# Raw q and k in long runs, and a token order that follows: a clustered attention and mixture-of-experts kernel

## The chip, the cores and the metric

The kernel runs on one core of a Trainium2 chip (trn2). The metric is the time of one execution in microseconds of the device, median of the runs; the kernel before takes 701.96 us (three runs, 701.67 to 702.21). TensorE does the matrix products and the 128x128 transposes, VectorE (DVE) and ScalarE (ACT) work on elements, GpSimd (POOL) helps them, and SyncE (SP) issues nearly all DMAs, in one queue. Sixteen DMA engines move the bytes.

## What is computed

Attention in clusters, then a dense layer, then a mixture of experts. The part that the change touches is the attention: 2 batches of 8 heads, 768 tokens, 64 dimensions.

```python
q_assign = argmax(einsum('bhsd,hcd->bhsc', q_n, c_n))      # 16 centroids per head
k_assign = argmax(einsum('bhsd,hcd->bhsc', k_n, c_n))
mask = q_assign[:, :, :, None] == k_assign[:, :, None, :]
scores = where(mask, 0.125 * q @ k.T, -1e9)
attn = softmax(scores)
out = attn @ v
x = out.transpose(0, 2, 1, 3).reshape(B * S, H * D)
h = x @ w_in;  x = (h * sigmoid(h)) @ w_out
out[n] = gate[n] * (relu(x[n] @ w1[e]) @ w2[e])            # e: the expert of token n
```

Nothing in the attention depends on the order of the tokens, as long as q, k, v, the masks and the place of the output use the same one.

## The kernel before

The heads are worked on in eight pairs, two heads at a time; here they are called pair 1 to pair 8 (p = 0 to 7 in the code). Pair 1 is treated apart, to start early: `head` loads its q and k with tokens on the partitions, and TensorE transposes them. For pairs 2 to 8 `quarter` loads q and k so that VectorE can transpose them: q of a pair is four DMAs, one for each head and half of the 64 dimensions, and each goes to 32 partitions of the tile `rawq`. Partition j of the 32 gets, for each of 24 blocks g of 32 tokens, 32 elements of token 32g + j: 768 pieces of 128 bytes for one DMA. The same holds for k (`rawk`). GpSimd scales q by 0.125 in place (`fq`), and `fdt` transposes half of the tokens in 32x32 blocks into `full`, with dimensions on the partitions and tokens along them.

From `full` comes all that the scores need (`prep`, `tr`): a rounded high part and a low part of q and k (QQ, K1, lq, KX), and the cluster of each token, found by products with the centroids and a short chain on VectorE that ends in `clu_0oq`. Parts of these tiles have to lie on other partitions too, so SP copies them from SBUF to SBUF: seven copies a pair (six for pair 1), each of 64 partitions by 768 elements, from line 489, and for pairs 2 to 8 four copies of masks, each to 32 partitions, from line 555. The first scores of a pair need three of the seven copies: QX, QQ and K1 of its first head. In pair 1 SP issues these as first, second and fourth.

The scores of a pair are worked on in twelve chunks of 128 query tokens (`chunk_ops`): products on TensorE (lines 596 and 599), a row maximum on VectorE (618), the exponential on ScalarE (624), a transpose on TensorE (635), copies to SBUF, and then the products with v (701), six chunks of v tokens. The sums of the exponentials are turned over by a round trip through DRAM (`rsc`, then `rb`, lines 688 and 693), and line 706 (`fN`) multiplies by their inverses and writes the result, tokens along the free axis, into `xT`, from which the dense layer reads.

The order of all this is set at build time by a planner (`Sched`): each operation has an engine, a cost and a priority, and each engine gets its instructions in the order that the plan gives. What is planned is not what the chip does: the instructions wait for each other by semaphores. A DMA of SP also waits until the one eight places before it is done, since it takes over that one's semaphore. During the wait for pair 1's first scores TensorE does dummy products (line 304), a fixed number of them, ahead of the first scores in its order:

```python
warm(opts.get("warm2", 20), 1, 217, [scores], 50)
```

`whole` loads v of a pair in pieces of 256 bytes (a token of one head), 128 tokens at a time.

Of the kernel before, what the change touches and what calls it, by code (L numbers as in the profile page):

```python
# [187 lines left out]
P = 128  # L188
B, H, S, D = 2, 8, 768, 64
NPAIR = B * H // 2  # L190
NC6 = S // P
HALF = S // 2
# [28 lines left out]
def alt(engines, fn, n, psum=False, two=False):  # L221

    return [(e, cost(e, n, psum, two), (lambda e=e: fn(e)), e == "Pool" or e == "DVE" and not psum) for e in engines]
# [5 lines left out]
def attention(tc, sc, pools, q, k, v, centroids, ident, xT, opts):  # L229
    nc = tc.nc  # L230
    if True:
# [5 lines left out]
        def sbt(buf, shape, dt=F32, part=""):  # L237
            return pools["a_early" if buf.tag in EARLY else "a_sb"].tile(shape, dt, tag=buf.key + part, name=buf.key + part)

        def pst(buf, shape=(P, 512)):  # L240
            return pools["a_ps"].tile(list(shape), F32, tag=buf.key, name=buf.key)
# [95 lines left out]
        def load(p):  # L337
            b, hp = divmod(p, H // 2)
            r = raws[p] = {}
            base = 12.0 * (p - 1) - 12  # L340
            for n, (nm, src) in enumerate((("q", q), ("k", k), ("v", v))):
                buf = Buf("raw" + nm)

                def whole(src=src, buf=buf):
                    buf.tile = sbt(buf, [P, 2, NC6, D])
                    nc.sync.dma_start(buf.tile, src[b, 2 * hp:2 * hp + 2].rearrange("h (c p) d -> p h c d", c=NC6))

                def head(h, src=src, buf=buf):
                    if h == 0:
                        buf.tile = sbt(buf, [P, NC6, 2 * D])  # L350
                    nc.sync.dma_start(buf.tile[:, :, h * D:(h + 1) * D], src[b, 2 * hp + h].rearrange("(c p) d -> p c d", c=NC6))

                def quarter(a, src=src, buf=buf):
                    if a == 0:
                        buf.tile = sbt(buf, [P, S // 32, 32])
                    half = slice(32 * (a % 2), 32 * (a % 2) + 32)
                    nc.sync.dma_start(buf.tile[32 * a:32 * a + 32], src[b, 2 * hp + a // 2].rearrange("(g j) d -> j g d", j=32)[:, :, half])
                fs = [whole] if nm == "v" else [lambda h=h, f=head: f(h) for h in range(2)] if p == 0 else [lambda a=a, f=quarter: f(a) for a in range(4)]
                pr = base + 0.1 * n + (opts.get("rawp", 5.0) if p > 1 else 0)
                if p == 0 and nm == "v":  # L360
                    pr += opts.get("v0", 11.5)
                elif p == 1 and nm != "v":
                    pr = -23.0 + 0.1 * n
                deps = [raws[p - 1][nm][1]] if p > 1 or p and nm == "v" else []
                o = None
                for k_, f in enumerate(fs):
                    o = op("SP", 475 if p == 0 else 620, f, deps=[o] if k_ else deps, uses=[buf], alloc=[] if k_ else [buf], prio=pr, soft=k_ > 0,
                           xfer=1800 if nm == "v" else 900 if p == 0 else 640)
                    if k_ == 0:
                        start = o  # L370
                r[nm] = (buf, o)
                if p == 0 and nm == "v" or p == 2:
                    wait.append(start)

        def prep(p):

            base = 12.0 * (p - 1)
            hp = p % (H // 2)
# [6 lines left out]
            buf, lq = Buf("opn"), Buf("lq")  # L385
# [13 lines left out]
            if p:  # L399
                rq = raws[p]["q"]  # L400

                def fq():
                    t = rq[0].tile.rearrange("p a i -> p (a i)")
                    nc.gpsimd.tensor_scalar(t, t, 0.125, 1.0, ALU.mult, ALU.mult)
                scaled.append(op("Pool", 882, fq, deps=[rq[1]], uses=[rq[0]], prio=base, gated=True))

            def tr(nm, x, pr):

                rb, ro = raws[p][nm]
                mb, fb = Buf("t"), Buf("full")  # L410
                xs = slice(x * HALF, (x + 1) * HALF)
                HI = "QQ" if nm == "q" else "K1"
                new = [] if his else [buf, lq]

                def ft():
                    mb.tile = pst(mb)
                    for i in range(3):
                        nc.tensor.transpose(mb.tile[:, i * P:(i + 1) * P], rb.tile[:, 3 * x + i], ident)

                def fdt():  # L420
                    fb.tile = sbt(fb, [P, HALF])
                    nc.vector.transpose(fb.tile, rb.tile[:, 12 * x:12 * x + 12].rearrange("p a i -> p (a i)"))

                def fe(e):
                    fb.tile = sbt(fb, [P, HALF])
                    elems(nc, e, fb.tile, mb.tile[:, :HALF], scale=0.125 if nm == "q" else None)

                def fh(e):
                    mk()
                    elems(nc, e, tl[HI][:, :, xs], fb.tile.unsqueeze(1).to_broadcast([P, 2, HALF]))  # L430

                def fl(e):
                    elems(nc, e, tl["lq"][:, xs] if nm == "q" else tl["KX"][:, 0, xs], fb.tile, tl[HI].bitcast(F32)[:, 1, xs], ALU.subtract)

                def flk(h):
                    rs = slice(64 * h, 64 * h + 64)
                    return lambda e: elems(nc, e, tl["KX"][:64, h, xs], fb.tile[rs], tl[HI].bitcast(F32)[rs, 1, xs], ALU.subtract)
                o = ro
                if p == 0:
                    o = op("PE", 327, ft, deps=[o, o_id], uses=[mb, rb], alloc=[mb], prio=pr, gated=True)  # L440
                    o = op(alt(["Act", "DVE"], fe, HALF, psum=True), 0, None, deps=[o], uses=[mb, fb], alloc=[fb], prio=pr)
                else:
                    if nm == "q":
                        o = scaled[0]
                    o = op("DVE", 469, fdt, deps=[o] + (held["masks"] if p == 1 and his else []), uses=[rb, fb], alloc=[fb], prio=pr, gated=True)
                evs.append((fb, o))
                lead = p == 1 and not his
                his[nm, x] = o = op(alt(["DVE", "Act", "Pool"] if p == 0 else ["Act"] if lead else SPLIT_HI, fh, S), 0, None, deps=[o] + list(his.values())[:1] + (held["masks"] if lead else []),
                                    uses=[fb, buf, lq], alloc=new, prio=pr + (2 + 0.1 * (nm == "q") if p == 0 else 0))
                if p == 0 and nm == "k":  # L450
                    los[nm, x] = op(alt(["DVE", "Pool"], flk(0), HALF, two=True), 0, None, deps=[o], uses=[fb] + bufs[nm], prio=pr + 2.2)
                    lo1.append(op(alt(["Pool"], flk(1), HALF, two=True), 0, None, deps=[o], uses=[fb] + bufs[nm], prio=pr + 4.2))
                else:
                    los[nm, x] = op(alt(["DVE", "Pool"] if p == 0 else ["Pool"] if p == 1 and nm == "q" else SPLIT_LO, fl, HALF, two=True), 0, None, deps=[o], uses=[fb] + bufs[nm], prio=pr + (2.2 if p == 0 else 0))
# [126 lines left out]
        def chunk_ops(p, h, c, i, grp, both):  # L581
            o = ops[p]
            t = o["t"]
# [6 lines left out]
            g = i // 3  # L590
# [56 lines left out]
            if i < 2:  # L647

                a = op("PE", 355, fSa, deps=o["first"], uses=[sb, o["buf"]], alloc=[sb], prio=pf("S"), name=f"S{i}")
                a = Sops[i] = op("PE", 355, fSb, deps=[a] + o["ready"][h] + o["mq"][:1], uses=[sb, o["buf"]], prio=pf("S"), name=f"S{i}")  # L650
            else:
                a = Sops[i] = op("PE", 711, fS, deps=o["ready"][h] + o["mq"][:(1 + c // 3) if h == 0 else 4], uses=[sb, o["buf"]], alloc=[sb], prio=pf("S"), name=f"S{i}")
            a = op("DVE", 865, fM, deps=[a], uses=[sb, nb], alloc=[nb], prio=pf("M"), name=f"M{i}")
# [12 lines left out]
            if i % 3 == 2:  # L666
                b, hp = divmod(p, H // 2)
                x = c // 3
                col = x * HALF
                rows = (slice(0, 64), slice(64, 128))  # L670
                if x not in both:
                    both[x] = dict(r=Buf("rr"), grp={}, ops=[])
# [12 lines left out]
                rb, yb, scr = Buf("rb"), Buf("t"), rsc[2 * p + x]  # L685
# [17 lines left out]
                    return f  # L703

                def fN():
                    nc.vector.tensor_tensor(xT[b][hp][:, col:col + HALF].rearrange("m (j p) -> m j p", j=3),  # L706
                                            yb.tile[:, :HALF].rearrange("m (j p) -> m j p", j=3),
                                            rb.tile.rearrange("m p j -> m j p"), ALU.mult)
                r = op("SP", 1100, fW, deps=w["ops"], uses=[w["r"]], prio=pf("W"), xfer=opts["XW"], late=opts["WL"] * (p == 0), name=f"W{i}")
# [9 lines left out]
        i = 0  # L719
# [979 lines left out]
```

## Time and profile before

| | us |
|---|---|
| median of three runs | 701.96 |
| lowest and highest | 701.67, 702.21 |
| the profiled execution | 701.06 |
| its span (first to last instruction) | 699.2 |
| TensorE busy | 684.9 (98%) |
| VectorE busy | 506.8 (72%) |
| ScalarE busy | 416.8 (60%) |
| GpSimd busy | 126.5 (18%) |

The attention takes about the first 230 us; the dense layer and the experts follow. The page of the profile gives busy times by engine. The table of waits says how long an engine stood still for what; the timeline lists the instructions of an engine in order, a number of equal ones in one row, with the idle time before them in brackets; the windows give the busy time of each engine in a stretch, the clock granted to TensorE as a share of full speed, the share of time in which the 16 DMA engines were busy (packets that overlap count twice, so it can exceed 1) and what they moved.

### The profile page before, as it was taken

To read this page: it belongs to the slowest core of one execution; us is meant where nothing else is said; L and a number is where in the kernel's file an instruction comes from. 1 tells how busy PE (TensorE), PEld (TensorE's weight loads), DVE (VectorE), ACT (ScalarE), POOL (GpSimd) and SP (SyncE) were. 2 spreads that over 40 slices of the span, in tenths; PEclk is the share of its full clock that TensorE was granted. 3 is DMA by queue.
4 is the path that set the end of the run, shared out by engine and by line. 5 is a ranking of instruction groups with operands and counts; after the bars stand their busy time and mean duration, and the time that the engine had idled before them with its cause. 6 is when DMAs were issued, how large, how long until landed. Compare 5 with 4: busy or idle time off the path is not lost. (4 is left out here: it accounts for less than half of the span.)

```text
span 699.2 us, 11768 instructions
## 1 busy us (share of the span) xinstructions
PE 684.9 (98%) x4106; PEld 555.6 (79%) x4106; DVE 506.8 (72%) x977; ACT 416.8 (60%) x753; POOL 126.5 (18%) x158
## 2 busy tenths in 40 slices
PE   8999999999999999999999999999999999999995
PEld 7857777677676789999988999999878878787763
DVE  6878898887986789998469353332599888897730
ACT  5956777677777355555343243332555988896740
POOL 5421332232300000000003100000043315221011
PEclk9999999999999999999999999999999999999998
DMA  9964876752620677674204932000022688847740
GB/s 191 182 138 93 177 178 127 156 125 58 151 69 13 184 251 269 191 260 174 98 1 152 358 125 60 31 1 1 0 93 82 198 317 309 318 167 223 279 177 20
DMA packets 104338, 104.82 MB, mean 150 GB/s; under 512 B 70668, under 2 KB 75024, under 8 KB 104272
## 3 DMA queue, kind: packets, MB, share of 16 engines
q1 hardware_dynamic: 101728, 96.56, 48.0%
q0 software_dynamic: 2400, 7.41, 3.1%
q8 instruction: 34, 0.56, 0.4%
q14 instruction: 32, 0.26, 0.1%
q10 hardware_dynamic: 144, 0.03, 0.0%
HBM read 104.99 MB, written 15.17 MB: 172 GB/s over the span
## 5 line engine op out<-in xcount | busy, mean ns | idle before, releaser
L1304 PE MATMUL bank<-whl,whl 128*128 128x384 f32 x768 | 145.7, 338 | 0.6 <-DVE whl L200 0.6
L1304 PEld LDWEIGHTS bank<-whl,whl 128*128 128x128 f32 x768 | 135.5, 188 | 6.4 <-DVE whl L200 1.0
L200 DVE TENSOR_TENSOR whl<-w,whl 128x1024 fp32r<-128x1024 f32 (+2 forms) x100 | 112.6, 1165 | 7.1 <-ACT whl L202 6.4
L624 ACT ACTIVATE p<-big,nm 128x768 f32<-128x768 f32 x96 | 86.8, 905 | 35.2 <-DVE nm L618 33.4
L618 DVE TENSOR_REDUCE nm<-big 128x1 f32<-128x768 f32 x96 | 90.0, 951 | 15.8 <-PE big L599 14.7
L202 ACT ACTIVATE whl<-w 128x1024 fp32r<-128x1024 f32 (+2 forms) x96 | 94.6, 1027 | 8.9 <-DMA w<-in_moe_w_dram 3.1
L635 PE MATMUL t<-ident,p 128*128 128x128 f32 x576 | 75.9, 273 | 1.4 <-DVE w L706 1.4
L635 PEld LDWEIGHTS t<-ident,p 128*128 128x128 f32 x576 | 66.7, 141 | 10.1 <-issue 5.0
L1431 PE MATMUL bank<-whl,xb 128*128 128x512 f32 x288 | 73.2, 400 | 0.0
L1473 PE MATMUL bank<-whl,w 128*128 128x512 f32 x288 | 72.4, 398 | 0.0
L202 ACT ACTIVATE pt<-t 128x384 f32<-128x384 f32 x129 | 58.2, 493 | 20.1 <-PE t L635 20.0
L701 PE MATMUL t<-pt,rawv 128*64 128x384 f32 x384 | 68.3, 494 | 0.0
L1431 PEld LDWEIGHTS bank<-whl,xb 128*128 128x128 f32 x288 | 52.3, 188 | 13.1 <-issue 1.2
L1473 PEld LDWEIGHTS bank<-whl,w 128*128 128x128 f32 x288 | 52.6, 188 | 11.5 <-issue 0.8
L1081 POOL TENSOR_SCALAR row<-L,mx 128x8 f32<-128x8 f32 x12 | 4.6, 383 | 268.5 <-PE bank L1048 143.0
L701 PEld LDWEIGHTS t<-pt,rawv 128*64 128x64 f32 x384 | 25.0, 136 | 31.4 <-issue 31.2
L200 DVE TENSOR_TENSOR whl<-wraw,whl 128x1024 fp32r<-128x1024 f32 x31 | 38.0, 1225 | 15.0 <-ACT whl L202 15.0
L202 ACT ACTIVATE whl<-wraw 128x1024 fp32r<-128x1024 f32 x31 | 32.7, 1057 | 25.7 <-DVE wraw L942 21.9
L1345 PE MATMUL bank<-whl,g_0w 128*128 128x512 f32 x144 | 38.2, 392 | 0.0
L1345 PE MATMUL bank<-whl,g_2w 128*128 128x512 f32 x144 | 37.8, 394 | 0.0
L596 PE MATMUL big<-opn_0K,opn_0QQ 128*128 128x384 f32 x96 | 36.1, 380 | 1.4 <-ACT p L624 0.9
L1345 PE MATMUL bank<-whl,g_1w 128*128 128x512 f32 x144 | 37.2, 392 | 0.0
(301 smaller groups left out, 1095.0 us busy)
## 6 DMA issues: line engine op xcount, KB each, us to landing
w<-in_moe_w_dram SPq DMA_DIRECT2D x88, 512.0 KB
w<-in_moe_w_out_dram SPq DMA_DIRECT2D x8, 1024.0 KB
wraw<-wsc SPq DMA_DIRECT2D x16, 512.0 KB
wsc<-wraw SPq DMA_DIRECT2D x15, 512.0 KB
w<-in_moe_w_in_dram SPq DMA_DIRECT2D x7, 1024.0 KB
wraw<-in_moe_w_dram SPq DMA_DIRECT2D x8, 512.0 KB
x2d<-row SPq DMA_DIRECT2D x12, 260.0 KB
rawv<-in_v_dram SPq DMA_DIRECT2D x8, 384.0 KB
```

The source lines that it names most:

```text
L200: (nc.vector if e == "DVE" else nc.gpsimd).tensor_tensor(dst, a, b, op)
L202: nc.scalar.activation(dst, a, AF.Copy, scale=1.0 if scale is None else scale)
L596: nc.tensor.matmul(sb.tile[:, x, :HALF], t["QQ"][:, h, cs], t["K1"][:, h, sl(x)], start=True, stop=False)
L618: nc.vector.tensor_reduce(nb.tile, sb.tile[:, :, :HALF], AX.XY, ALU.max, negate=True)
L624: nc.scalar.activation(pb.tile.rearrange("p (a b) -> p a b", a=2), sb.tile[:, :, :HALF], AF.Exp, bias=nb.tile[:, 0:1], scale=1.0, accum_ou ...
L635: nc.tensor.transpose(tbs[x].tile[:, j * P:(j + 1) * P], pb.tile[:, kc * P:(kc + 1) * P], ident)
L701: nc.tensor.matmul(yb.tile[rows[z], :HALF], raws[p]["v"][0].tile[:, z, kc], w["grp"][z]["tile"][:, kc], start=(kc == 0), stop=(kc == NC6 - 1))
L1081: nc.gpsimd.tensor_scalar(xb.tile[:, DM:], L[:, j], mx[:, j:j + 1], 1.0, ALU.subtract, ALU.mult)
L1304: nc.tensor.matmul(hb.tile[:, :HALF], w[:, ws, dc, fs], xx[:, s, cs], start=(dc == 0 and n == 0), stop=(dc == 3 and n == 2))
L1345: nc.tensor.matmul(ab.tile, gb.tile[gs][:, js], w[:, ws, fc % 2], start=(fc == 0 and n == 0), stop=(fc == 15 and n == 2))
L1431: nc.tensor.matmul(hbs[x].tile, xs_[:, s, dc], w.tile[:, ws, x * 512:(x + 1) * 512], start=(dc == 0 and n == 0), stop=(dc == 3 and n == 2))
L1473: nc.tensor.matmul(ob.tile, hT.tile[:, s, fc * P:(fc + 1) * P], w.tile[:, ws, i * 512:(i + 1) * 512], start=(fc == 0 and n == 0), stop=(fc ...
```

## The change

Three things change together.

The quarters of q and k are loaded as runs: partition j of the 32 takes tokens 24j to 24j + 23 in one run of 24 x 64 elements less 32, that is 1,504 elements or 6,016 bytes. The run begins at the first or the second half of the dimensions, so of every 64 elements the first 32 are wanted and the other 32 are loaded too and not used. The tiles `rawq` and `rawk` become twice as large; a DMA has 32 runs.

Tokens get another order: place 128c + p along the free axis holds token 6p + c. `fdt` makes this order: it reads blocks at a stride and writes its elements four apart. Pair 1's q and k and all of v are loaded in that order too, so that a partition's six tokens lie next to each other in DRAM; v then has runs of 1,536 bytes. Pair 1's q and k still go to two interleaved places in their tile, in pieces of 256 bytes.

`fN` undoes the order: it writes every sixth element of `xT`, which so keeps the tokens in their own order.

```diff
@@ -343,18 +343,19 @@
 
                 def whole(src=src, buf=buf):
                     buf.tile = sbt(buf, [P, 2, NC6, D])
-                    nc.sync.dma_start(buf.tile, src[b, 2 * hp:2 * hp + 2].rearrange("h (c p) d -> p h c d", c=NC6))
+                    nc.sync.dma_start(buf.tile, src[b, 2 * hp:2 * hp + 2].rearrange("h (p c) d -> p h c d", c=NC6))
 
                 def head(h, src=src, buf=buf):
                     if h == 0:
-                        buf.tile = sbt(buf, [P, NC6, 2 * D])
-                    nc.sync.dma_start(buf.tile[:, :, h * D:(h + 1) * D], src[b, 2 * hp + h].rearrange("(c p) d -> p c d", c=NC6))
+                        buf.tile = sbt(buf, [P, 4 * NC6, D])[:, :2 * NC6].rearrange("p (c h) d -> p c (h d)", h=2)
+                    nc.sync.dma_start(buf.tile[:, :, h * D:(h + 1) * D], src[b, 2 * hp + h].rearrange("(p c) d -> p c d", c=NC6))
 
                 def quarter(a, src=src, buf=buf):
                     if a == 0:
-                        buf.tile = sbt(buf, [P, S // 32, 32])
-                    half = slice(32 * (a % 2), 32 * (a % 2) + 32)
-                    nc.sync.dma_start(buf.tile[32 * a:32 * a + 32], src[b, 2 * hp + a // 2].rearrange("(g j) d -> j g d", j=32)[:, :, half])
+                        buf.tile = sbt(buf, [P, 4 * NC6, D])
+                    at, n = 32 * (a % 2), S * D // 32 - 32
+                    nc.sync.dma_start(buf.tile.rearrange("p a d -> p (a d)")[32 * a:32 * a + 32, :n],
+                                      src[b, 2 * hp + a // 2].rearrange("(j n) d -> j (n d)", j=32)[:, at:at + n])
                 fs = [whole] if nm == "v" else [lambda h=h, f=head: f(h) for h in range(2)] if p == 0 else [lambda a=a, f=quarter: f(a) for a in range(4)]
                 pr = base + 0.1 * n + (opts.get("rawp", 5.0) if p > 1 else 0)
                 if p == 0 and nm == "v":
@@ -400,7 +401,7 @@
                 rq = raws[p]["q"]
 
                 def fq():
-                    t = rq[0].tile.rearrange("p a i -> p (a i)")
+                    t = rq[0].tile[:, :, :32]
                     nc.gpsimd.tensor_scalar(t, t, 0.125, 1.0, ALU.mult, ALU.mult)
                 scaled.append(op("Pool", 882, fq, deps=[rq[1]], uses=[rq[0]], prio=base, gated=True))
 
@@ -419,7 +420,8 @@
 
                 def fdt():
                     fb.tile = sbt(fb, [P, HALF])
-                    nc.vector.transpose(fb.tile, rb.tile[:, 12 * x:12 * x + 12].rearrange("p a i -> p (a i)"))
+                    nc.vector.transpose(fb.tile.rearrange("p (c j a) -> p c a j", c=3, a=4),
+                                        rb.tile.rearrange("p (a c) d -> p c a d", c=NC6)[:, 3 * x:3 * x + 3, :, :32])
 
                 def fe(e):
                     fb.tile = sbt(fb, [P, HALF])
@@ -666,7 +668,6 @@
             if i % 3 == 2:
                 b, hp = divmod(p, H // 2)
                 x = c // 3
-                col = x * HALF
                 rows = (slice(0, 64), slice(64, 128))
                 if x not in both:
                     both[x] = dict(r=Buf("rr"), grp={}, ops=[])
@@ -703,7 +704,7 @@
                     return f
 
                 def fN():
-                    nc.vector.tensor_tensor(xT[b][hp][:, col:col + HALF].rearrange("m (j p) -> m j p", j=3),
+                    nc.vector.tensor_tensor(xT[b][hp].rearrange("m (p c) -> m c p", c=NC6)[:, 3 * x:3 * x + 3],
                                             yb.tile[:, :HALF].rearrange("m (j p) -> m j p", j=3),
                                             rb.tile.rearrange("m p j -> m j p"), ALU.mult)
                 r = op("SP", 1100, fW, deps=w["ops"], uses=[w["r"]], prio=pf("W"), xfer=opts["XW"], late=opts["WL"] * (p == 0), name=f"W{i}")
```

No engine's instructions change their order or number. SP's queue at the start of the program, from the first quarter of pair 2 (`rawq_217`, `rawk_239`) to the last copy of pair 1 (`opn_0...`), before:

```order
3 L357 DMA rawq_217<-in_q_dram 32x24x32 x4
4 L357 DMA rawk_239<-in_k_dram 32x24x32 x4
5 L489 DMA opn_0QX<-opn_0QQ 64x768
6 L489 DMA opn_0QQ<-lq_259 64x768
7 L489 DMA opn_0QX<-opn_0QQ 64x768
8 L489 DMA opn_0K_256<-opn_0K_256 64x768
9 L489 DMA opn_0QQ<-lq_259 64x768
10 L489 DMA opn_0K_256<-opn_0K_256 64x768
```

and with the change:

```order
3 L357 DMA rawq_217<-in_q_dram 32x1504 x4
4 L357 DMA rawk_239<-in_k_dram 32x1504 x4
5 L491 DMA opn_0QX<-opn_0QQ 64x768
6 L491 DMA opn_0QQ<-lq_259 64x768
7 L491 DMA opn_0QX<-opn_0QQ 64x768
8 L491 DMA opn_0K_256<-opn_0K_256 64x768
9 L491 DMA opn_0QQ<-lq_259 64x768
10 L491 DMA opn_0K_256<-opn_0K_256 64x768
```

Nothing moved: the eight quarters still stand ahead of the six copies, in another shape.

VectorE at the start of pair 2, with the change (`clu_0` are pair 1's clusters, `full_316` and `full_335` pair 2's transposed q):

```order
27 L517 STREAM_TRANSPOSE clu_0t<-clu_0e 128x384
28 L423 STREAM_TRANSPOSE full_316<-rawq_217 128x3x4x32
29 L525 SCALAR_TENSOR_TENSOR clu_0oq<-t_282,clu_0t 128x384
30 L565 TENSOR_SCALAR opn_0KX<-clu_0oq,hrow,hneg 32x384 x2
31 L423 STREAM_TRANSPOSE full_335<-rawq_217 128x3x4x32
32 L620 TENSOR_REDUCE nm_352<-big_337 128x1
```

Here too only the transposes' shape is another (128x384 before); the transpose of pair 2's q still stands ahead of the instruction that ends pair 1's chain.

## Rows read from the trace of the kernel before

**Rows 1.** The page's head: span and busy time, its share and instructions by engine.

```profile
span 699.2 us, 11768 instructions
...
PE 684.9 (98%) x4106; PEld 555.6 (79%) x4106; DVE 506.8 (72%) x977; ACT 416.8 (60%) x753; POOL 126.5 (18%) x158
```

**Rows 2.** TensorE's table of waits: total us, times, longest us.

```profile
PE t L635 <- DVE w L706: 1.4, 1, 1.4
```

**Rows 3.** TensorE's timeline at two waits for DMAs: start, us, what, [idle, releaser].

```profile
6.88 0.84 PE L418 MATMUL t<-ident,rawk 128*128 128x128 f32 x6 [1.12 <-DMA rawk<-in_k_dram]
...
89.99 0.41 PE L599 MATMUL big<-opn_1KX,opn_1QX 96*128 96x384 f32 x1 [0.19 <-DMA opn_1KX<-clu_0ok]
```

**Rows 4.** Windows: us, busy (x instructions) of five engines, PEclk, DMA share, GB/s.

```profile
2.00:5.40 3.40, 3.40 (x22) 3.30 (x21) 2.65 (x16) 0.73 (x3) 0.98 (x11) 1.00 1.18 238
5.70:9.90 4.20, 3.08 (x22) 1.89 (x22) 2.27 (x5) 3.79 (x8) 2.40 (x3) 1.00 1.13 163
10.30:15.10 4.80, 4.63 (x38) 4.30 (x37) 4.08 (x8) 2.31 (x5) 2.06 (x3) 1.00 0.99 234
13.00:37.00 24.00, 22.74 (x151) 18.50 (x152) 20.18 (x35) 22.11 (x47) 9.62 (x13) 1.00 0.97 180
71.00:90.00 19.00, 18.66 (x128) 14.04 (x126) 17.24 (x31) 14.94 (x33) 6.02 (x9) 1.00 0.82 180
157.90:160.60 2.70, 2.70 (x21) 2.56 (x20) 2.37 (x6) 2.67 (x7) 0.98 (x2) 1.00 0.70 146
584.40:591.10 6.70, 6.70 (x90) 5.43 (x89) 4.72 (x8) 5.30 (x10) 4.38 (x2) 1.00 0.99 397
691.50:693.80 2.30, 0.03 (x2) 0.00 (x0) 0.00 (x0) 0.47 (x1) 0.98 (x1) 1.00 0.01 4
693.80:699.20 5.40, 0.00 (x0) 0.00 (x0) 0.00 (x0) 0.00 (x0) 0.00 (x0) 0.50 0.07 21
```

**Rows 5.** TensorE's timeline at the start and at pair 2's first use of masks.

```profile
1.06 3.80 PE L304 MATMUL t<-wz 128*128 128x128 f32 x18 [1.06 <-DVE wz L268]
...
9.07 2.94 PE L304 MATMUL t<-wz 128*128 128x128 f32 x24
...
14.50 0.58 PE L596 MATMUL big<-opn_0K,opn_0QQ 128*128 128x384 f32 x2 [0.17 <-issue]
...
37.73 0.34 PE L599 MATMUL big<-opn_1KX,opn_1QX 96*128 96x384 f32 x1
```

**Rows 6.** SP's timeline at the start: start, us over all its DMAs, what.

```profile
3.04 3.19 SPq L357 DMA_DIRECT2D rawq<-in_q_dram  x4
6.28 2.27 SPq L357 DMA_DIRECT2D rawk<-in_k_dram  x4
8.67 0.65 SPq L489 DMA_DIRECT2D opn_0QX<-opn_0QQ  x1
...
10.69 0.54 SPq L489 DMA_DIRECT2D opn_0K<-opn_0K  x1
```

**Rows 7.** SP's timeline from 32 us on, and line 706 on VectorE's.

```profile
32.70 1.22 SPq L555 DMA_DIRECT2D opn_1KX<-clu_0ok  x2
...
34.60 5.38 SPq L357 DMA_DIRECT2D rawk<-in_k_dram  x4
...
40.65 1.14 SPq L693 DMA_DIRECT2D rb<-rsc  x2
...
45.12 0.66 DVE L706 TENSOR_TENSOR w<-t,rb 128x384 f32<-128x384 f32 x1 [2.10 <-DMA rb<-rsc]
```

**Rows 8.** DMA issues: what, how many, KB each.

```profile
rawq<-in_q_dram SPq DMA_DIRECT2D x28, 96.0 KB
```

**Rows 9.** Groups of VectorE, 0 to 240 us: busy us, mean ns, idle before.

```profile
L618 DVE TENSOR_REDUCE nm<-big 128x1 f32<-128x768 f32 x96 | 90.0, 951 | 15.8 <-PE big L599 14.7
...
L706 DVE TENSOR_TENSOR w<-t,rb 128x384 f32<-128x384 f32 x16 | 10.6, 665 | 14.2 <-PE t L701 11.9 <-DMA rb<-rsc 2.1
...
L422 DVE STREAM_TRANSPOSE full<-rawq 128x384 f32<-128x384 f32 x14 | 7.6, 554 | 0.0
```

## The prediction, made before the change was run

> **What bounds the kernel now.** I read the page's head first: a span of 699.2 us, TensorE busy for 684.9 us of it (98%), the next engine, VectorE, for 72% [rows 1]. So only what makes TensorE idle counts, and in its table of waits the longest is 1.4 us on VectorE's line 706 [rows 2]; beside the waits for other engines only two are for DMAs, 1.12 us for the load of k of pair 1 and 0.19 us for a mask copy [rows 3]. The profiled execution took 701.06 us, 1.9 us around its span, 0.90 us below the median of 701.96; I make the sum against 701.06 and move it by 0.90. About 0.2%, or 1.4 us, is what a measurement of this kernel can tell from no change.
>
> In the first 90 us the DMA engines are the second bound. The windows by stretch [rows 4] show a DMA share of 1.13 while the eight quarters of pair 2 (the first pair with quarters) pass, 0.99 while the copies of pair 1 follow, 0.97 from 13 to 37 us. All these transfers go through SP's one queue, and a copy behind the quarters waits for them to drain. The reader should see three places where that queue meets TensorE:
> - *The first scores, at 14.50.* TensorE's timeline [rows 5] shows dummy products and, 0.17 us after them, the first score product. It needs the copies of QX, QQ and K1, the first, second and fourth copy that SP issues, from 8.67 to 10.69, behind eight quarters issued from 3.04 to 8.55 [rows 6]. Were these copies late or early? The four loads of pair 1 (786,432 bytes) began at about 2.0, at 238 GB/s [rows 4] end near 5.3, and released TensorE at 6.88 [rows 3]: about 1.5 us from the last bytes to the release. The quarters (4.82 us, below) end near 10.1; four copies of 196,608 bytes at 234 GB/s take 3.4 us; with 1.5 us that is 15.0, against a start of 14.50. So the K1 copy has no slack.
> - *The wait of 1.4 us near 45* [rows 2]. TensorE waits for line 706, which waited 2.10 us for rb. SP shows why: four k quarters from 34.60 on took 5.38 us to issue, and rsc and rb stand behind them [rows 7].
> - *The masks of pair 4, at 89.99*: TensorE waited 0.19 us for them [rows 3], so they have no slack.
>
> **The change, part by part.**
> *Quarters.* 56 DMAs (28 of q, 96.0 KB each [rows 8], and as many of k) become 32 runs of 6,016 bytes, 192,512 bytes: nearly twice the bytes, 32 descriptors instead of 768. SP's order is unchanged. The old cost is in a row: 163 GB/s, so 98,304 bytes in 0.60 us, eight in 4.82. The new one is in none. From below: weights, 128 partitions and runs of 4 KB, move at 397 GB/s, and eight new quarters would take 3.88 us (0.94 less). From above: the mask copies, which write 32 partitions as a quarter does, move at 146 GB/s: 10.55 us (5.73 more) [rows 4]. The nearest rows are two: the copies of Q and K, 64 partitions with the queue full, at 234 GB/s (6.58 us), and the masks per busy engine time, 146 at a share of 0.70, so 209 (7.37 us). I take the middle, 6.97 us: 2.15 more for eight, 0.27 for each.
>
> What the rows show is that few partitions go with 146 to 234 GB/s, and 128 partitions with 397. The Trainium skill states a rule for it (SBUF — State Buffer, "Door 1: The DMA port swizzle"): partitions 0 to 63 reach no more DMA ports than 0 to 31, half of the sixteen, and it gives about 218 GB/s for them. By that figure the eight quarters would take 7.06 us, an estimate; the trace agrees, with 234 and 146 to 209, but holds no load from HBM to 32 partitions.
>
> (a) First scores: K1 has no slack, so +2.15 us; ends -0.17 (then the dummy products hold it) and +5.7. (b) Pair 2's scores: ahead of its masks in the queue stand, in SP's order, twelve more quarters (eight of pair 3, four of pair 4), 12 x 0.27 = 3.2 us, less about 0.3 for each of two v loads (256-byte runs become 1,536 bytes, and long runs to 128 partitions are the faster ones [rows 4]). Against it: 0.7 us in which the queue was idle from 13 to 37 (share 0.97) and the masks' slack: their issue ends at 33.92 [rows 7], they are used at 37.73 [rows 5], and if they land 2.7 us after their issue (rb took 3.3 us behind four quarters, to 45.12 from an issue that ended at 41.79 [rows 7]) that is 1.1 us. Net +0.8; ends 0 and +3.2. (c) The wait near 45: TensorE comes there 2.95 us later, and the four k quarters ahead of rb cost 1.1 us more, so rb is early: -1.4; ends -1.4 and 0. What is late next there is nothing that the waits name. (d) Pair 4's masks: eight quarters stand ahead of them in SP's order of the 20 us before, 2.15 us if the queue were always full; its share is 0.82 from 71 to 90, and the quarters start from an idle queue, so I take half, +1.1; ends -0.19 and +2.15. The later pairs have their masks earlier and appear in no wait.
>
> *VectorE.* 28 transposes (554 ns) now read strided blocks and write every fourth element; 16 products of line 706 write every sixth. Line 706 already reads rb at a stride of three elements and takes 665 ns [rows 9]; that is 111 ns above those transposes. From below the new strides cost nothing, from above 111 ns x 44 = 4.9 us. I cost them at nothing: VectorE waited 14.7 us for TensorE before its reductions of line 618 alone [rows 9], which is the cover. Without it they would add up to 4.9 us. At the start a transpose stands ahead of the steps that make pair 1's masks; 0.1 us there hides behind (a). GpSimd's scaling of q reads 32 of 64 elements at a time, with as many elements, and no engine waits for it: nothing.
>
> *v and pair 1.* The v loads wait for nobody in the table of waits. Pair 1's loads still write pieces of 256 bytes, so the 1.1 us for k stays.
>
> Sum: 2.15 + 0.8 - 1.4 + 1.1 = +2.65 us. 701.06 + 2.65 = 703.7 for the profiled execution, **704.6 us** in terms of the median.
>
> **The rivals.**
> *The bytes pile up.* If a late K1 lets TensorE idle for longer than the 2.3 us that it was idle in the tail with the clock still at 1.00, before it fell to 0.50 [rows 4], its clock may fall to 1.2 GHz. The first 18 passes of the kernel took 211 ns each, later ones 122 [rows 5]: 18 x 89 ns = 1.6 us. With (d) in full (+1.05 more) and (b) half way to its end (+1.2) this gives 704.6 + 3.85 = 708.5. For it: delays add up in one queue whose share is 0.97 from 13 to 37; against it: the share of 0.82 from 71 to 90, which leaves room.
> *The runs are fast.* It decides at 319 GB/s: above that the new eight take no longer than the old 4.82 us. Then (a) is 0 or -0.17, (b) 0, (c) -1.4, (d) -0.19: 701.96 - 1.6 or 1.76, so 700.3. For it: four quarters took 5.38 us to issue where four others took 2.27 [rows 6, 7]. The Trainium skill speaks for it (DMA: Bandwidth & Descriptors, "Specifications": 512 bytes or more for line rate); that rule by itself would give this time. Against it: the rates for few partitions [rows 4].
> *It cancels.* At some 280 GB/s eight quarters take 5.5 us: (a) +0.7, (b) 0, (c) -1.4, (d) +0.3, so 701.6, no change. That the change does not do what it says is no rival: the new shapes stand in SP's queue.
>
> **How the numbers follow.** Forecast, slower by 2.65 us: 0.48. Piled up: 0.20. Fast runs: 0.17. Cancelled: 0.15. Of the forecast's own spread (a at 1.76 to 2.55, d from 0 to 2.15, so 703.1 to 706.0) a little lies within 1.4 us: same 0.17, faster 0.17, slower 0.66. The range holds the fast case's 700.3 at its lower end and the piled-up case's 708.5 at its upper: 700.3 to 708.5. The forecast's own range is 703.1 to 706.0.
>
> **What would show it.** Right: the first score product near 16.7 with the wait before it put down to a DMA; the stretch of the eight quarters at 200 to 235 GB/s; no wait on line 706 near 48; a longer wait for masks near 93. Wrong: the first score at 14.5, or quarters above 319 GB/s; a wait on VectorE in the steady pairs; or transposes well above 665 ns with TensorE waiting for them.

## Result and profile after

The changed kernel takes 707.3 us (median of 6), the one before 701.8: a ratio of 1.0079 with a 95% interval of 1.0055 to 1.0104, so 5.5 us slower (3.9 to 7.3). I had said 704.6. The profiled execution took 707.06 us, and its span is 6.0 us longer than that of [rows 1].

The page's head and TensorE's table of waits after the change (total us, times, longest), against [rows 1, 2]:

```profile
span 705.2 us, 11769 instructions
...
PE 687.2 (97%) x4106; PEld 557.4 (79%) x4106; DVE 512.8 (73%) x977; ACT 417.0 (59%) x753; POOL 126.0 (18%) x158
```

```profile
PE t L637 <- DVE w L707: 2.6, 1, 2.6
PE big L598 <- DMA opn_0K<-opn_0K: 2.1, 1, 2.1
PE t L419 <- DMA rawk<-in_k_dram: 1.7, 1, 1.7
PE big L598 <- ACT p L626: 1.2, 3, 0.7
```

TensorE is busy 2.3 us longer for the same work, most of it (1.9 us) where its clock was lower, as the windows below show; the other 3.7 us are waits. The first line is the wait that I expected to go. TensorE's timeline at the places of [rows 3, 5], then windows with the columns of [rows 4]:

```profile
7.85 0.85 PE L419 MATMUL t<-ident,rawk 128*128 128x128 f32 x6 [1.72 <-DMA rawk<-in_k_dram]
...
17.44 0.59 PE L598 MATMUL big<-opn_0K,opn_0QQ 128*128 128x384 f32 x2 [2.14 <-DMA opn_0K<-opn_0K]
...
41.96 0.41 PE L601 MATMUL big<-opn_1KX,opn_1QX 96*128 96x384 f32 x1
...
79.51 0.44 PE L598 MATMUL big<-opn_0K,opn_0QQ 128*128 128x384 f32 x1 [0.67 <-ACT p L626]
```

```profile
2.00:5.40 3.40, 3.40 (x18) 3.25 (x17) 2.90 (x17) 0.64 (x2) 0.97 (x11) 1.00 0.88 198
5.70:14.10 8.40, 6.68 (x52) 5.13 (x51) 5.39 (x10) 4.73 (x10) 4.70 (x5) 1.00 1.04 234
13.00:37.00 24.00, 21.34 (x132) 18.19 (x131) 18.87 (x31) 19.26 (x41) 9.45 (x14) 0.93 1.05 222
18.90:22.20 3.30, 3.30 (x14) 2.93 (x13) 1.40 (x3) 2.71 (x6) 1.17 (x2) 0.50 1.04 228
71.00:90.00 19.00, 18.33 (x123) 13.80 (x125) 16.71 (x27) 13.94 (x30) 6.14 (x9) 1.00 0.72 169
```

The first score starts at 17.44 instead of 14.50. The stretch of the quarters runs at 234 GB/s and lasts to 14.1. After TensorE stood still for 2.14 us its clock fell from 2.4 to 1.2 GHz (0.50 from 18.9 to 22.2). From 13 to 37 the DMA share is 1.05 where it was 0.97. In steps of 2 us it is never below 0.99 now; before, it fell to 0.84 from 23 to 25 and to 0.42 from 35 to 37. Where this text says that the queue has gaps, it means such stretches in which the share falls.

SP and VectorE around line 707, to [rows 7], and VectorE's groups, to [rows 9] (busy us, mean ns, idle before):

```profile
39.53 3.09 SPq L357 DMA_DIRECT2D rawk<-in_k_dram  x4
...
43.20 1.14 SPq L694 DMA_DIRECT2D rb<-rsc  x2
```

```profile
50.49 0.84 DVE L707 TENSOR_TENSOR w<-t,rb 128x384 f32<-128x384 f32 x1 [3.24 <-DMA rb<-rsc]
```

```profile
L620 DVE TENSOR_REDUCE nm<-big 128x1 f32<-128x768 f32 x96 | 89.9, 949 | 17.0 <-PE big L601 16.3
L707 DVE TENSOR_TENSOR w<-t,rb 128x384 f32<-128x384 f32 x16 | 13.9, 871 | 14.4 <-PE t L702 11.1 <-DMA rb<-rsc 3.2
L423 DVE STREAM_TRANSPOSE full<-rawq 128x384 f32<-128x384 f32 x14 | 12.2, 893 | 0.0
```

SP was free to issue rb, at 43.20 to 44.34, just after the sums that rb reads back had landed (43.09), yet rb came only at 50.4. The transposes went from 554 to 893 ns, the products from 665 to 871.

How late each kernel is against the kernel before, read at the same reductions (start of nm<-big of the n-th of 96 score chunks, us; one execution each, worked out from the traces):

```
chunk  before at  after  bytes_only  halves_all  strides_only  hybrid  before_rb_first
    0      15.47   2.96        3.74        0.98          1.06    0.84             0.23
   11      34.10   4.03        3.73        1.39          1.49    1.27             0.25
   12      38.47   4.30        6.28        1.38          1.47    3.07             0.24
   20      57.88   5.55        6.30        0.29          0.05    3.75            -1.33
   28      74.46   6.39        6.30        1.12          0.88    4.53            -1.33
   95     220.53   6.04        5.97        2.37          4.28    5.00            -0.46
```

The steps of the column "after" are the account of the loss: 2.96 at the first score, about 1.1 by chunk 11, 0.27 at pair 2's start, 1.25 at line 707, 0.83 near 79, -0.35 by the end: 6.0.

Each column is one execution, and the executions of one kernel differ: the twelve of *halves_pair2* took 701.5 to 709.1 us. The columns of *strides_only* and *hybrid* are the slowest execution of each (706.96 and 707.42). The end of the program, from VectorE's last instruction on, lies behind everything that the change touches; it took 17.2 us in the profiled executions before and after, and 18.9 and 18.6 in those two.

### The profile page after: what moved, and what is told of

Its sections match the earlier page's. It is cut to its first block, busy times and chain, and to the rows that moved or that the text cites. A ratio compares the mean times of both kernels' runs of the same rounds, so it can differ in the third digit from the quotient of the medians.

```text
span 705.2 us, 11769 instructions
## 1 busy us (share of the span) xinstructions
PE 687.2 (97%) x4106; PEld 557.4 (79%) x4106; DVE 512.8 (73%) x977; ACT 417.0 (59%) x753; POOL 126.0 (18%) x158
## 5 line engine op out<-in xcount | busy, mean ns | idle before, releaser
L626 ACT ACTIVATE p<-big,nm 128x768 f32<-128x768 f32 x96 | 86.8, 905 | 40.0 <-DVE nm L620 36.9
L1474 PEld LDWEIGHTS bank<-whl,w 128*128 128x128 f32 x288 | 52.6, 188 | 11.5 <-issue 0.8
```

Of the source, the lines that this page charges most:

```text
L626: nc.scalar.activation(pb.tile.rearrange("p (a b) -> p a b", a=2), sb.tile[:, :, :HALF], AF.Exp, bias=nb.tile[:, 0:1], scale=1.0, accum_ou ...
L1474: nc.tensor.matmul(ob.tile, hT.tile[:, s, fc * P:(fc + 1) * P], w.tile[:, ws, i * 512:(i + 1) * 512], start=(fc == 0 and n == 0), stop=(fc ...
```

## The experiments

Ratios are to runs of the kernel before on the same chip, us by that ratio on 701.7. In the cuts of code `...` stands for what is left out.

**Bytes or strides?** *bytes_only*, on the kernel before:

```diff
+at, n = 32 * (a % 2), S * D // 32 - 32
+nc.sync.dma_start(buf.tile...[32 * a:32 * a + 32, :n], src...rearrange("(j n) d -> j (n d)", j=32)[:, at:at + n])
...
-nc.vector.transpose(fb.tile, rb.tile[:, 12 * x:12 * x + 12]...)
+nc.vector.transpose(fb.tile, rb.tile...[:, x * HALF:x * HALF + HALF])
```

> The kernel before (its token order, its v loads, its products, its contiguous VectorE transposes), with the quarters of pairs 2 to 8 as runs of 6,016 bytes to 32 partitions. The transposes and the scaling read the first 768 elements of each row of the tile, contiguous, instead of the strided blocks, so q and k of pairs 2 to 8 hold the wrong features; as much is computed as before. Theory A, the bytes: first score near 16.9 (2.45 us for the quarters on the 14.50 of before), a clock fall after it, and a time 3.5 to 5 us above the kernel before, 705.3 to 706.8. Theory B, the VectorE strides: no more than 1.5 us above it.

Measured: 1.0070 (1.0049 to 1.0090), 4.9 us. Its first score:

```profile
17.55 0.98 PE L597 MATMUL big<-opn_0K,opn_0QQ 128*128 128x384 f32 x2 [2.45 <-DMA opn_0K<-opn_0K]
```

Pair 2's masks came late next:

```profile
PE big L600 <- DMA opn_1KX<-clu_0ok: 2.3, 1, 2.3
```

The long loads alone, with VectorE untouched (its transposes take 554 ns), cost nearly the whole loss, but partly at another place: chunk 12 steps by 2.55 at the masks, and line 707's counterpart does not make TensorE wait.

*halves_all*, on the change:

```diff
+half = slice(32 * (a % 2), 32 * (a % 2) + 32)
+nc.sync.dma_start(buf.tile[32 * a:32 * a + 32, :, :32], src...rearrange("(j n) d -> j n d", j=32)[:, :, half])
```

> The change as it is (its token order, its strided VectorE and GpSimd work, its v loads), but each quarter moves only the 32 features that are used, as 768 pieces of 128 bytes to the same places of the same tile (98,304 bytes instead of 192,512). Theory A, the doubled bytes in SP's one queue make the loss: the first score comes back from 17.44 to 15.5 at most (what stays is pair 1's later loads, 0.97 us), TensorE's clock stays up after it, the wait behind line 707 near 51 shrinks to about the 1.4 us of before, and the time is within 2 us above the kernel before: 702.0 to 704. Theory B, the strided VectorE work makes it (its transposes went from 554 to some 900 ns, its products from 665 to 870): the time stays near that of the change, 706.5 to 707.5.

Measured: 1.0033 (1.0018 to 1.0049), 2.3 us; first score at 15.48, TensorE's wait for line 707's counterpart 0.3 us. The bytes are most of it, but 2.3 us stay.

*strides_only*, halves_all with pair 1 as in pair1_old below:

> The change with the quarters as 128-byte pieces (98,304 bytes each) for all pairs and pair 1 in the token order of before: of the change only the token order of pairs 2 to 8 is left, with VectorE's strided transposes and products and the v loads in 1,536-byte runs. Theory A (the queue makes the loss; the strided VectorE work costs some): the first score is back at 14.5 to 14.8, and what is left is 0.8 us near 75 where TensorE waits for the exponentials, and up to 1.4 us at the masks of pair 4: 702.0 to 703.5. Rival, strides cost nothing at all: within 0.5 us of the kernel before.

Measured: 1.0030 (1.0018 to 1.0043), 2.1 us. The first score was missed, 15.56: this load writes 128-byte pieces to rows of 256 bytes, and its eight quarters took 5.35 us after pair 1's k, not 3.95. By chunk 20 that delay is gone (0.05). What follows is 0.83 near 74, and then

```profile
92.57 0.41 PE L600 MATMUL big<-opn_1KX,opn_1QX 96*128 96x384 f32 x1 [2.21 <-DMA opn_1KX<-clu_0ok]
```

SP issued these masks from 86.6 to 89.2, 2.4 us later than in the kernel before (84.1 to 86.8). Pair 4's transposes stand at the head of the chain to them, but the clusters at its end came only 0.6 us later (83.17 instead of 82.57); SP's queue in front of the masks was already 1.4 us late, and the sums there (`rsc`) took 2.61 us to issue instead of 1.79. Whether the transposes or the load into rows of 256 bytes made that is not shown, so the 2.1 us are not the price of VectorE's strides alone. In this execution the clock fell behind that wait (0.55 from 93 to 96), which adds about 1.6 us from chunk 36 to 40 and is the main reason why its column ends at 4.28, above the median of 2.1. That strided work costs nothing falls: the 0.83 near 74 is a wait for exponentials behind longer transposes.

*half_runs*, on bytes_only:

```diff
-at, n = 32 * (a % 2), S * D // 32 - 32
+at, n = 32 * (a % 2), S * D // 64
```

> The kernel before, with each quarter of pairs 2 to 8 loaded as 32 runs of 3,072 bytes: the 98,304 bytes of before in the long form. A partition gets 12 tokens of 64 features instead of 24 of 32, and the transposes and the scaling read them contiguous, so q and k of those pairs hold the wrong features; as much is computed as before. Theory A, bytes into 32 partitions count: at the 233 GB/s of the change's quarters one takes 0.42 us, against 0.60 before and 0.79 to 0.83 with 6,016-byte runs; the first score is not later than the 14.50 of before (dummy products hold it at 14.3), and the time is 700.5 to 702. Rival, the form itself (one descriptor per partition) sets the pace whatever it carries: quarters stay near 0.79 us, the first score near 17, and the time 705 or more.

Measured: 0.9983 (0.9971 to 0.9995), 1.2 us faster than before:

```profile
14.50 0.59 PE L597 MATMUL big<-opn_0K,opn_0QQ 128*128 128x384 f32 x2
```

Its eight quarters landed at 7.25 to 9.59, one every 0.33 us, 294 GB/s; those of the change at 8.57 to 14.11, one every 0.79 us, 243 GB/s. The form, 32 descriptors a quarter, is good; the doubled bytes spoil it. That 32 partitions set the rate was not tried: all quarters here go to 32.

**The start.** *halves_pair2*: the load of halves_all under `if p == 1:`, the long one otherwise.

> The change, with the eight quarters of pair 2 alone moved as 768 pieces of 128 bytes each to the same places; pairs 3 to 8 keep their runs of 6,016 bytes. It parts the start from the rest. Theory A, the start (quarters ahead of the copies of pair 1, then TensorE's clock) is most of the loss: first score at 15.0 to 15.5, no clock fall, 2.5 to 3.5 us below the change, 703.8 to 704.8, and the wait behind line 707 near 50 stays at 2 us or more. Rival: TensorE only comes earlier to the same later queue waits (masks of pair 2, rb near 50), which then grow: less than 1.5 us below the change.

Measured: 1.0044 (1.0023 to 1.0064), 3.1 us, 2.4 below the change; first score 15.59, no fall of the clock. But line 707's counterpart did not wait at all: rb had landed at 43.9. The late rb comes from the backlog built at the start as well, not from its four quarters alone.

*pair1_old*, on the change:

```diff
-src...rearrange("h (p c) d -> p h c d", c=NC6)
+src...rearrange("h (c p) d -> p h c d" if p == 0 else "h (p c) d -> p h c d", c=NC6)
...
-src...rearrange("(p c) d -> p c d", c=NC6)
+src...rearrange("(c p) d -> p c d", c=NC6)
...
-xT[b][hp].rearrange("m (p c) -> m c p", c=NC6)
+xT[b][hp].rearrange("m (c p) -> m c p" if p == 0 else "m (p c) -> m c p", c=NC6)
```

> The change, with pair 1 (q, k, v and its product with rb) in the token order of before: the loads of q and k of pair 1 again read pieces of 256 bytes. Theory C, the loads of pair 1 are slower in the new order (rows of 256 bytes were at 238 GB/s from 2 to 5.4 us, those of the change at 198) and everything behind them in the queue is 0.97 us late: the first score at 16.5, 1 us below the change, 706.3. Rival: the lag is chance or made by the queue behind them: the first score stays at 17.4 and the time within 0.5 us of the change, 707.3.

Measured: 1.0053 (1.0037 to 1.0069), 3.7 us; the interval overlaps that of the change, so a gain in time is not shown. The first score came at 16.27, and pair 1's loads ran at 232 GB/s from 2 to 5.4 us again. Over all the traces, pair 1's k landed at 6.99 to 8.26 in the six kernels with its new order, and at 6.75 to 6.86 in seven of the eight with the old one (7.42 in *bytes_only*). The new order delays it, by an amount that varies.

*more_warm*, on the change:

```diff
-for _ in range(m):
+for _ in range(m + more):
...
-... lambda i=i: f(i == 0), ...
+... lambda i=i: f(i == 0, 17 * (n > 20 and i == 20)), ...
```

> The change with 17 more dummy products on TensorE ahead of the first score product (26 instead of 9 after the product with tri), about 1.9 us of the 2.1 us in which it waits there for the K1 copy. Theory: that wait lets the granted clock fall to 0.50 from 18.85 to 22.26, which cost 1.1 us; with the dummies the clock stays at 1.00 after 17.4, and the time is 1.1 us below the change, 706.0. Rival: the fall comes from something earlier in the start, or what it cost is hidden behind the masks of pair 2 at 42: no gain, 707.0 to 707.5.

Measured: 1.0103 (1.0084 to 1.0123), no gain. The clock stayed at 1.00, but I gave too many dummies: the edit took hold in two groups of them, so 34 were added and not 17 (52 in a row instead of 18). K1 landed at 17.02, the dummies ended at 18.5, and the first score started at 18.52.

At chunk 11 it is 4.43 us late, 0.40 more than the change, from a first score 1.08 later: so the fall cost about 0.7 us. At rb it lost less than the change (0.36 against 1.25 by chunk 20), and at the masks of pair 4 more; by chunk 95 both are 6.1 us late.

**Both parts undone.** *hybrid*, pair1_old and halves_pair2 together:

> The change with pair 1 in the token order of before (q, k, v, product with rb) and the quarters of pair 2 as 128-byte pieces; pairs 3 to 8 as in the change. Both parts of the late start are undone at once. Theory A: first score at 14.5 to 14.8, no clock fall, rb there before TensorE needs it near 46 (as with pair 2 alone, where it landed at 43.9), which gains the 1.35 us that the kernel before waits there; 0.8 us is lost near 75 where TensorE waits for the exponentials; in sum about 0.5 us below the kernel before: 700.5 to 702.5. Theory B, the strided VectorE work by itself costs more than that: 703 or more.

Measured: 1.0054 (1.0033 to 1.0074), 3.8 us: theory A's time was missed, and its first score too, at 15.34. In the profiled execution, the slowest of six, theory B's reason is the smaller part: about 1.2 of the 5.0 us are waits for exponentials, and two waits for late transfers follow the first score:

```profile
40.71 0.41 PE L604 MATMUL big<-opn_1KX,opn_1QX 96*128 96x384 f32 x1 [1.54 <-DMA opn_1KX<-clu_0ok]
...
49.58 0.55 PE L640 MATMUL t<-ident,p 128*128 128x128 f32 x3 [2.04 <-DVE w L710]
```

In this execution the full queue decides and not the start. A transfer has landed when all of its 16 parts have; the times of the last parts after the first, for the quarter that lands near 33 us (not the same one in each kernel) and for the first copy of pair 2's masks KX (us, from the trace's completions):

```
                first part   15th    16th  | mask KX: first   15th    16th
before              32.60   +0.44   +0.52  |         34.64   +0.24   +0.26
after               33.31   +1.26   +2.88  |         39.77   +1.33   +2.05
halves_pair2        33.53   +0.36   +1.00  |         37.66   +0.25   +0.91
hybrid              33.22   +1.03   +2.86  |         38.10   +0.94   +2.47
```

In the kernels that wait, the last part comes 2 to 3 us after the first, and 0.7 to 1.8 us of that after the fifteenth: it looks as if one of the sixteen DMA engines runs late, though the trace does not name the engines. In the kernel before one part was also late, by 1.9 us at 24, and had caught up by 27.6, where the share falls. Under the change it does not fall from 13 to 37 us, and the lag stays. The kernel before is not free of it either: when its rb is due the lag is back, and the last parts of pair 4's k quarters come up to 3.9 us after the first (36.60 to 40.46).

*hybrid_contig*, on the hybrid:

```diff
-nc.vector.transpose(fb.tile.rearrange("p (c j a) -> p c a j", c=3, a=4),
+nc.vector.transpose(fb.tile.rearrange("p (c a j) -> p c a j", c=3, a=4),
...
+for a in range(4):
+    nc.sync.dma_start(buf.tile[32 * a:32 * a + 32], src...rearrange("h (j a c) d -> a j h c d", a=4, c=NC6)[a])
...
+xT[b][hp].rearrange("m (j a c) -> m c a j", a=4, c=NC6)[:, 3 * x:3 * x + 3]
```

> The same, with the columns of pairs 2 to 8 ordered so that VectorE's transposes write contiguous blocks of 32 (token 24j+6a+c at column 128c+32a+j); v follows in four transfers of 32 partitions a pair, and the product with rb writes every 24th element. Theory: the write at every fourth element is what took the transposes from 554 to 900 ns; they come back to 550 to 620 ns, and TensorE's four waits for the exponentials near 75 (1.9 us in halves_all) go: 0.3 to 0.8 us below the hybrid. Rival: the strided reads are the cost: 850 ns or more, and the same time as the hybrid or up to 1 us above it, from the v transfers.

Measured: 1.0063 (1.0043 to 1.0084), no better than the hybrid, with the transposes as expected:

```profile
L431 DVE STREAM_TRANSPOSE full<-rawq 128x384 f32<-128x384 f32 x14 | 7.6, 552 | 0.0
```

Reading strided blocks of 32 costs nothing; writing every fourth element costs 340 ns. TensorE's waits for exponentials fell from 1.9 to 1.1 us in all. The product went the other way, to 1,071 ns, and masks of pair 2 made TensorE wait 2.44 us.

**Place in the queue.** *before_rb_first*, on the kernel before:

```diff
+if p == 3 and nm in ahead:
+    deps = deps + ahead[nm]
...
 r = op("SP", 1200, fB, deps=[r], uses=[rb], alloc=[rb], ...)
+if p == 0 and x == 0:
+    ahead["k"] = [r]
```

> The kernel before; the first k quarter of pair 4 waits in the planner for the rb transfers of pair 1's first group, so that SP issues rsc, rsc, rb, rb ahead of it (the order of what follows shifts with it). Theory: rb waits in the queue behind four quarters, and TensorE for rb: the 1.35 us wait near 45.8 goes, with 0.8 us more there, as in the run with runs of 3,072 bytes, which was 2.16 us earlier from there on: 699.3 to 700.2. Rival: pair 4's k then comes too late for its copies, or the wait moves to the masks: no gain, 701 or more.

Measured: 0.9978 (0.9964 to 0.9992), 1.5 us faster than before and 7 us faster than the change: the best version here that computes the reference, small as it is. Line 706's counterpart no longer waits for rb:

```profile
37.67 1.14 SPq L695 DMA_DIRECT2D rb<-rsc  x2
```

```profile
43.18 0.67 DVE L708 TENSOR_TENSOR w<-t,rb 128x384 f32<-128x384 f32 x1
```

Of the 1.6 us gained there, 0.9 went again at pair 4's masks (a wait of 1.13 us at 89.6).

*after_rb_first*, the same on the change:

> The same on the change: rb ahead of the four long k quarters of pair 4. Theory: the 2.59 us wait on line 707 near 51 is the price of these quarters ahead of rb; it goes or falls under 0.5 us, and the time comes down by 1.5 to 2.6 us, to 704.7 to 706. Rival: TensorE comes earlier to the masks of pair 4 or the copies of pair 3, which the same full queue delays: less than 0.8 us of gain.

Measured: 1.0038 (1.0023 to 1.0052), 2.7 us: 2.8 below the change, slightly more than forecast. The wait fell from 2.6 to 1.0 us. SP issued rb only at 44.36, when the sums that it reads back had landed (44.34): their last part came 2.9 us after the fifteenth. About 0.8 us of what this execution gained lies ahead of rb, at chunk 11 (3.23 late instead of 4.03): its clock fell earlier, from 8.2 to 11.5, and the dummy products that followed took up the delay.

*after_order*, on after_rb_first:

```diff
+if p == 1:
+    ahead["q"] = mops[-4:]
```

> The same, and the four q quarters of pair 4 wait for the mask copies of pair 2 as well, which SP then issues ahead of them. Theory: masks that stand behind four long quarters land 3.2 us later than they need to; pair 2's scores start 1 to 3 us earlier than in the change (its first maximum was at 42.8), and the time is 0.5 to 2 us below the run with rb alone. Rival: pair 2's start is set by something else (operands or the chain of exponentials), no more than 0.3 us of gain over rb alone.

Measured: 1.0035 (1.0024 to 1.0046), no difference from rb alone. Pair 2's start in it was 2.1 us earlier than in the change, but so was its first score, by 1.2. Masks alone are not shown to cost anything.

## Why the prediction was right and where it was wrong

Right was the sign and the cause: twice the bytes, in the one queue that the copies, masks and rb share, at about the rate that the neighbouring rows gave (243 GB/s, where 319 would have been needed to gain by my count of the old quarters and 390 by their landings). Half_runs and bytes_only show the bytes; that 32 partitions set the rate stays an argument. The time lies in the range, outside the forecast's own 703.1 to 706.0: the change cost 5.5 us where I added up 2.65. It lies near the rival "the bytes pile up", but that is luck: none of that rival's three additions came as it had them (the clock 1.6, (b) and (d) larger), and others took their place. Of my signs of being right, the wait on line 706 did not go and the one for masks near 93 did not come; of those of being wrong, transposes above 665 ns with TensorE waiting for them came. By its steps, in the profiled execution:

- **(a), +2.15, was 2.94.** The quarters took 6.40 us instead of 3.95 from the landing of pair 1's k on (2.45 more; I had 4.82 and 6.97 from a window that began earlier), the copies behind them 0.47 less, and pair 1's loads came 0.96 later. "The 1.1 us for k stays" was wrong: it became 1.72. The new order is a cause of that (see pair1_old), but in other executions with this order the wait was 0.2 to 2.1. That K1 had no slack was right: it had landed at 14.26 in the kernel before, for a first score at 14.50.
- **The clock, only in a rival, fell**, behind 2.14 us of idle time, less than the 2.3 us that the rival asked for. The price was 0.7 us, not 1.6.
- **VectorE at nothing was wrong.** TensorE lost 0.42 by chunk 3 and 0.83 near 79, both waits for exponentials (the first read from halves_all and strides_only, since in the change the fall of the clock lies over it). Bytes_only, with its transposes at 554 ns, loses neither, and hybrid_contig, at 552, not the first. The idle time of line 618, 14.7 us over 96 reductions, is no cover at the few places where transposes stand in front of a reduction. In the change two longer transposes stand ahead of the reduction at 24.48, and three ahead of that at 77.44. My upper bound of 111 ns each was also too low: 340 and 206.
- **(b), +0.8, was 0.27**, on top of a start already 4 us late; in bytes_only the same term was 2.55. The 0.3 us that it took off for each v load came from no row: the first took 1.58 us from the landing in front of it, before 1.72. **(d), +1.1, was about -0.2** (chunks 34 to 36 in the traces; -0.35 by the end): TensorE came later than the masks.
- **(c), -1.4, is the step that failed: it was +1.25**, the largest single error. I let TensorE come 2.95 us later and rb 1.1, the price of four quarters by themselves. TensorE came about 4.3 us later, but rb landed 5.4 us later (50.37 instead of 45.00). SP was not blocked: its four k quarters took 3.09 us to issue instead of 5.38. But the last of them landed at 49.22 instead of 41.93, and rb, behind them, took 6 to 7 us from issue to landing instead of 3.8. They are twice the size, they stood behind what was left of the start, and parts of them were late: of rb's 16 parts the fifteenth, too, came over 2 us after the first. After_rb_first and halves_pair2 both take the wait down, from its two sides, and halves_all, with half the bytes, to 0.3 us.

The terms do not add up one by one. Bytes alone cost 4.9 us, and what strides_only keeps costs 2.1; together they cost 5.5: what one loses early, the other does not lose again.

## What to carry over

When a load is made of fewer and longer descriptors, count the bytes that it moves, used or not, and then follow the queue to every small transfer behind it. Here a copy or a row of sums paid for everything that was still in front of it when SP issued it. Where the queue had gaps a delay was gone soon (1.9 us within 4 us), and where it had none it reached the next consumer; so look at the stretches' DMA share before trusting a landing time of before. And idle time summed over a kernel covers nothing at the one place where an operation gets longer.

## What was not expected

- A transpose on VectorE that writes every fourth element takes 893 instead of 554 ns; one that reads blocks of 32 out of rows of 64 and writes contiguously 552.
- Runs of 3,072 bytes into 32 partitions moved at 294 GB/s, those of 6,016 bytes at 243. The Trainium skill (SBUF — State Buffer, "Door 1: The DMA port swizzle") gives about 218 GB/s for so few partitions; both are above it. The eight quarters go to four groups of 32 partitions in turn, and which of them overlapped was not read.
- The last part of the transfers fell behind the first by 1.1 to 1.6 us at a time. Each such step from 17 to 30 us in the traces of after and hybrid coincides with a packet of kind "instruction" (at 22.48 for 1.30 us and at 27.55 for 0.72 us in after); the kernel before has such packets too, at 17.42 and 22.29. That these packets push a DMA engine back was not tried.
- TensorE's clock fell to 0.50 at the end of 2.14 us of idle time before the first score or soon after it, and likewise with waits of 2.45 and 2.31 us in bytes_only, 2.44 in hybrid_contig, 2.21 in strides_only and 2.10 in after_rb_first. With the 2.59 us at line 707 it did not (1.00 from 51.4 to 54), nor with the 2.04 us in hybrid.
